# Attention backward beside a ReGLU: gradient products one slot behind the scores, another order of the first loads

## The chip, the cores and the metric

The kernel runs on one core of a Trainium2 chip. The metric is the device time of one execution in microseconds (us); the median of several runs is given. A core has five engines with instruction streams of their own, in the rows of the profile: PE (TensorE, matrix products; its weight loads are shown as PEld), DVE (VectorE), ACT (ScalarE), POOL (GpSimd) and SP (SyncE, which here only issues DMAs). `SPq` and `ACTq` are the DMA issues of SP and ACT.

## The reference

A gated mix of sliding-window attention and a ReGLU layer, forward and all gradients, in bfloat16. S = 2048 rows, D = 512, H = 32 heads of Dh = 16, window 256, F = 1376.

```python
g = sigmoid((x * gate_w).sum(-1, keepdims=True))
q, k, v = split(x @ wqkv)                             # 32 heads of 16
scores = q @ k.T * Dh**-0.5                           # per head; 0 <= i - j < 256, else -1e9
a = (softmax(scores) @ v) @ wo
b = (relu(x @ W_gate) * (x @ W_up)) @ W_down
out = g * a + (1 - g) * b
# returned: out and the gradients of x, wqkv, wo, W_gate, W_up, W_down, gate_w for a given grad_out
```

For the attention gradient one needs, for each block of queries and keys, P = exp(scores), the product dP = dO V^T, and P * dP (called Pd in the kernel), row sums of both, and both once more with rows and columns exchanged.

## The kernel before

**First stage (0 to about 250 us): the ReGLU.** A step is one chunk of 128 features (`fc`, 11 of them) for one group of 512 rows (`tg`, 4 of them): N1 = 44 steps. The loop over n runs 8 slots longer, and in slot n the parts of several steps are interleaved with a lag: `gate` and `up` of step n, `turn_h` of n - 1, `dh` of n - 2, stores of hT (`keep`) of n - 3, `turn_dgu` and stores of dgT and duT of n - 4, weight gradients of n - 6. `gate` makes a product in PSUM and ACT writes its ReLU to `rg` (L368); `up` makes a second product, from which DVE makes `upm` (L374) and POOL `hT` (L376); `dh` makes a third, which ACT copies (L382) and which DVE and POOL turn into the halves of `dgu` (L385, L386). `rg`, `upm`, `hT` and `dgu` go round in four buffers each. `keep` issues its three stores from ACT's queue (L399), and the transposes `turn_h` (L390) and `turn_dgu` (L394) are DMAs issued by SP. `turn_x` transposes the next group's x on PE. Before the loop SP issues the first loads in a written order: both halves of the first group of x, the first 128 columns of W_gate, the second group of x, gate_w, the first 128 columns of W_up, grad_out, and so on.

Near the end of this stage the projections of the first group of attention (Q, dO, K, V and their transposes; `project_parts`, L133 and L136 are its matmuls) are interleaved, and three parts of the second group (Q, dO, and the DMA transpose of their rows) at n = N1+4, N1+5, N1+6.

**Second stage (about 252 to 720 us): attention.** The work is a list of 360 units: for each of 4 column groups `c` (8 heads each) and 16 query blocks `j`, the key blocks j-1, j, j-2 (roles m, d, f: middle, diagonal, far), each in two halves of 4 heads. One slot of the loop does, by a written order, parts of several units:

- `front(units[n])`: the scores matmul ST (L680), its exp on ACT into `Pu` (L690), and for roles d and f the mask on POOL (L692, L695);
- `gradp(units[n - 1])`: the DVE product Pd = Pu * dPT (L709);
- `flip(units[n - 2])`: the exchange of rows and columns of P and Pd by a DMA transpose that SP issues (L737);
- `rowsum(units[n - LAG])`, LAG = 3: row sums into BA (L718, L720). Units without a DMA transpose are exchanged here on PE (L747) and copied out;
- `front_dp(units[n])`: the matmul dPT (L704), behind the row sums, or ahead of them where a new query block begins;
- then as credit allows `cd_piece` (L540, L543, the products with the exchanged P), parts of the next group's projections, and background products of the weight gradient (L634).

ST and dPT share a ring of four PSUM buffers:

```python
ST = ps.tile([P, HH, P], F32, tag="M", bufs=4, name="ST")
u.dPT = ps.tile([P, HH, P], F32, tag="M", bufs=4, name="dPT")
```

When the last row sum of a block is done, ACT copies BA (L724), and small operations follow on DVE (reciprocal L764) and POOL (ndel L767, rq L768 to L773, rows_st L775 to L782). `late` holds loads of weights for the last stage, `early` the first loads of attention gradients for it; the loop takes one of each now and then.

**Last stage (about 720 us to the end):** the outputs and the gradient of x, in 16 blocks of 128 rows (L1015 to L1098), on PE nearly all the time.

Of the kernel before, what the change touches and what calls it, by code (L numbers as in the profile page):

```python
# [11 lines left out]
BF = mybir.dt.bfloat16  # L12
# [10 lines left out]
def kernel(  # L23
# [20 lines left out]
    nc = tc.nc  # L44
    P = 128
# [152 lines left out]
    with ExitStack() as p1, tc.manual_schedule():  # L198
# [13 lines left out]
        def rows_of(ap, tg):  # L212
            return ap[tg * TGW:(tg + 1) * TGW, :].rearrange("(t p) d -> p t d", p=P)
# [28 lines left out]
        half = TPG // 2  # L242
        for i in range(2):
            nc.sync.dma_start(x_r[:, i * half:(i + 1) * half, :], rows_of(x_d, 0)[:, i * half:(i + 1) * half, :])
        gw_r = fp.tile([P, P], BF, tag="upm", name="gw_r")
        nc.vector.memset(tiny[:], 0.0)
        nc.vector.memset(gw_r[:], 0.0)
# [10 lines left out]
            nc.sync.dma_start(Wg_sb[:, :, a:b], Wg_v[:, :, a:b])  # L258
            nc.sync.dma_start(Wu_sb[:, :, a:b], Wu_v[:, :, a:b])

        nc.sync.dma_start(Wg_sb[:, :, 0:W0], Wg_v[:, :, 0:W0])
        load_x(1)
        nc.sync.dma_start(gw_r[0:DC, :], gate_w.rearrange("(c p) -> c p", p=P))
        nc.sync.dma_start(Wu_sb[:, :, 0:W0], Wu_v[:, :, 0:W0])
        load_go(0)
        nc.sync.dma_start(wd0[:], B_W_down[0:P, :])
        load_x(2)
# [89 lines left out]
        def tile1(tag, bufs=4):  # L357
            return fp.tile([P, TGW], BF, tag=tag, bufs=bufs, name=tag)
# [11 lines left out]
        def up(k):  # L370
            ups = ps1.tile([P, TGW], F32, tag="mm", bufs=3, name="ups")
            product(ups, lambda c: Wu_sb[:, c, k.fsl], lambda c: x_T[k.tg][:, c, :])
            k.upm, k.hT = tile1("upm"), tile1("hT")
            nc.vector.scalar_tensor_tensor(out=k.upm[:], in0=k.rg[:], scalar=0.0, in1=ups[:],  # L374
                                           op0=ALU.is_gt, op1=ALU.mult)
            nc.gpsimd.tensor_tensor(out=k.hT[:], in0=k.rg[:], in1=k.upm[:], op=ALU.mult)  # L376

        def dh(k):
            dhps = ps1.tile([P, TGW], F32, tag="mm", bufs=3, name="dhps")
            product(dhps, lambda c: WdT[k.fc][:, c, :], lambda c: db_T[:, c, k.ts])  # L380
            dh_sb = tile1("dh_sb", 2)
            nc.scalar.copy(dh_sb[:], dhps[:])  # L382
            k.dgu = fp.tile([P, 2, TGW], BF, tag="dgu", name="dgu")
            k.dgT, k.duT = k.dgu[:, 0, :], k.dgu[:, 1, :]
            nc.vector.tensor_tensor(out=k.dgT, in0=dh_sb[:], in1=k.upm[:], op=ALU.mult)  # L385
            nc.gpsimd.tensor_tensor(out=k.duT, in0=dh_sb[:], in1=k.rg[:], op=ALU.mult)  # L386
# [60 lines left out]
        for n in range(N1 + 8):  # L447
            at = lambda lag: steps[n - lag] if 0 <= n - lag < N1 else None
            if at(0):
                gate(at(0))  # L450
                if 0 < n < NTG:
                    gate_col(n)
                if n == 2:
                    turn_wd0()
                if n + 1 < NTG:
                    turn_x(n + 1)
                if n == 0:
                    turn_gw()
                up(at(0))
                if n == 0:  # L460
                    gate_col(n)
                if n < NTG:
                    db_rows(n)
                if at(0).tg == 0 and at(0).fc > 0:
                    turn_wd(at(0).fc)
            if 1 <= n <= NTG:
                turn_db(n - 1)
            if at(2):
                dh(at(2))
            if at(1):  # L470
                turn_h(at(1))
            if at(3):
                keep(at(3), (hT_d, at(3).hT[:]))
            if at(4):
                turn_dgu(at(4))
                keep(at(4), (dgT_d, at(4).dgT), (duT_d, at(4).duT))
            if at(6):
                f = weights(at(6))
                if f is not None:
                    stores[n + 1] = f  # L480
            if n in stores:
                stores.pop(n)()
            t = n - DA0
            if t % 2 == 1 and 0 <= t // 2 < NT:
                make_da(t // 2)
            if t % 2 == 0 and 0 < t // 2 <= NT:
                turn_da(t // 2 - 1)
            if t == 2:
                nc.vector.reduce_sum(par[:, 0:1], par4[:], axis=AX.X)
                nc.vector.tensor_scalar(par[:, 1:2], par[:, 0:1], -1.0, 1.0, op0=ALU.mult, op1=ALU.add)  # L490
            if n == NTG + 1:
                nc.scalar.activation(tiny[:], tiny[:], ACT.Exp)
            if t in (NT + 3, 2 * NT + 1):
                i = (t - NT - 3) // (NT - 2)
                nc.gpsimd.memset(zt[i][:, 0, :, :, :], 0.0)
                nc.vector.memset(zt[i][:, 1, :, :, :], 0.0)
            if n == N1 - 2:
                first = project_parts(*groups[0])
            for _ in range({N1 + 1: 2, N1 + 2: 0}.get(n, 1)):
                if first:  # L500
                    first.pop(0)()
            if n == N1 + 3:
                second = project_parts(*groups[1])
            if n in (N1 + 4, N1 + 5, N1 + 6):
                second.pop(0)()
            z = n - DA0 - NT - 2
            if z == 0:
                load_w(0)
            if z % 4 == 3 and 0 < z // 4 + 1 < DC:
                load_w(z // 4 + 1)  # L510

    p3 = ctx
    if True:
# [141 lines left out]
        for c in range(DC):  # L655
            for j in range(NT):
                kbs = [k for k in (j - 1, j, j - 2) if k >= 0]
                for half in range(2):
                    order = kbs if half or len(kbs) < 3 else [kbs[0], kbs[2], kbs[1]]
                    for ki, kb in enumerate(order):  # L660
                        u = Unit()
                        u.c, u.j, u.kb, u.half = c, j, kb, half
                        u.first = ki == 0 and half == 0
                        u.last = ki == len(kbs) - 1 and half == 1
                        u.role = ("d", "m", "f")[j - kb]
                        u.pair = u.role == "d" or (u.role == "m" and (c < DC - 1 or j in (3, 5, 7, 9)))
                        u.own = u.role == "f" or (u.role == "m" and half == 1 and not u.pair and j < 10)
                        u.dma = u.pair or (u.role == "m" and half == 0 and (c < DC - 1 or j < 10))
                        units.append(u)
        NU = len(units)  # L670
# [58 lines left out]
        def flip(u):  # L729
# [3 lines left out]
            if u.dma:  # L733
                if u.pair and u.half == 0:
                    return
                hs = slice(0, 2) if u.pair else slice(u.half, u.half + 1)
                nc.sync.dma_start_transpose(out=P2[key][:, hs, :, :, :].rearrange("p b a h q -> p (b a h) q"),  # L737
                                            in_=pairs.pop((u.c, u.j, u.kb))[:, hs, :, :, :].rearrange("p b a h q -> p (b a h q)"))
                for b in range(2)[hs]:
                    P2[(u.c, u.j, u.kb, b)] = P2[key][:, b, :, :, :]  # L740
                return
# [103 lines left out]
        with tc.manual_schedule():  # L845
# [3 lines left out]
            prq = []  # L849
            credit = 1.2  # L850
            SLOT = 1.5
            LAG = 3
            n = 0

            held = False
# [27 lines left out]
            while n <= NU + LAG or ev or cdq or bgq:  # L883
# [21 lines left out]
                for eng, f in now:  # L905
                    if eng == "pool":
                        f()
                if 1 <= n <= NU:
                    gradp(units[n - 1])
                for eng, f in now:  # L910
                    if eng == "dve":
                        f()
                for eng, f in now:
                    if eng == "pool+":
                        f()
                if 2 <= n < NU + 2 and units[n - 2].dma:
                    flip(units[n - 2])
                w = units[n - LAG] if LAG <= n < NU + LAG else None
                if u is not None and w is not None and w.first:
                    front_dp(u)  # L920
                    pieces()
                if w is not None:
                    rowsum(w)
# [2 lines left out]
                    if w.last:  # L926
# [5 lines left out]
                        for kb in done:  # L932
                            qbs = range(kb, min(NT, kb + 3))
                            for qb in qbs:
                                for half in range(2):
                                    e = n + (1 if qb < w.j else 5)
                                    cdq.append((e, w.c, kb, qb, half, qb == qbs[-1] and half == 1))
                if u is not None and not (w is not None and w.first):
                    front_dp(u)
                credit += SLOT - 0.63 - (0.44 if LAG <= n < NU + LAG and not units[n - LAG].dma else 0.0)  # L940
                if not (u is not None and w is not None and w.first):
                    pieces()
                if n >= NU:
                    if bgq:
# [20 lines left out]
                    credit -= 0.65  # L965
                if u is not None and u.c == DC - 1 and not bgq and u.j > 6 and "T0" not in S2:
                    early = early_group()
                if late and (u is None or u.c == 0 or (n % 12 == 1 and 3 <= u.j <= 8 if u.c < DC - 1 else
                                                       n % 4 == 1 and 1 < u.j < 10 or n % 2 and u.j > 9)):
                    late.pop(0)()  # L970
                if early and (u is None or n % 2 == 0 and u.j >= (9 if len(early) > 4 else 14)):
                    early.pop(0)()
                credit = max(-1.0, min(1.2, credit))
                for eng, f in now:
# [154 lines left out]
```

## Time and profile before

| | before |
|---|---|
| runs, us | 912.45, 912.24, 914.48 |
| median, us | 912.45 |
| the profiled execution, us | 913.61 |
| its span in the profile, us | 911.9 |
| granted TensorE clock | 1.00 |
| DMA, mean over the span | 185 GB/s |
| L704 dPT, 360 matmuls | 135.9 us, 378 ns each |
| L690 exp of the d units, 126 | 75.8 us, 601 ns each |
| L692 mask of the d units, 126 | 80.7 us, 641 ns each |
| L709 product of the d units, 126 | 85.8 us, 681 ns each |

The span is the part of the execution that the profile covers; what lies around it is 1.7 us here. In a line of the timeline the columns are start, duration, engine, source line, operation, output <- input, and in square brackets the idle time of the engine just before, with what ended it. In the list of waits they are the waiting operation, what ended the wait, the sum in us, the number of waits and the longest. Matmuls are pipelined: the next can begin before the bar of the previous one ends. Which event released a waiting instruction is inferred by the profile.

### The profile page before, as it was taken

How to read it: one execution, taken by the hardware profiler on the slowest of the kernel's cores; microseconds unless marked ns; L12 is line 12 of the kernel's file. 1: busy time of each engine (PE TensorE's matmuls, PEld its weight loads, DVE VectorE, ACT ScalarE, POOL GpSimd, SP SyncE). 2: the span in 40 equal slices, each digit the busy share in tenths (PEclk: the TensorE clock that was granted, in tenths of full speed). 3: DMA queues.
4: the chain of work that ended last, by engine and by line, in shares of the span. 5: the costliest groups of instructions: out<-in, count | busy, mean ns of one | idle time of the engine just before them, and what ended most of it. 6: DMA issues, size and time to landing. Idle time of an engine off the chain costs nothing.

```text
span 911.9 us, 26209 instructions
## 1 busy us (share of the span) xinstructions
PE 896.2 (98%) x10711; PEld 567.3 (62%) x10711; DVE 510.9 (56%) x952; ACT 441.6 (48%) x778; POOL 495.2 (54%) x937
## 2 busy tenths in 40 slices
PE   8999999999989999999999999999999999999998
PEld 5565665655647767667776677766777644444445
DVE  4433334434278877768777787776787222333333
ACT  6422222222268777667776677766688211000001
POOL 4554445545267777857878578875677212222221
PEclk9999999999999999999999999999999999999999
DMA  9989879999689999999999989999998999777731
GB/s 302 192 183 200 189 187 208 219 221 207 164 154 152 176 178 182 198 173 153 183 176 192 188 160 184 180 184 181 186 202 154 247 270 227 182 186 180 184 88 46
DMA packets 505577, 169.07 MB, mean 185 GB/s; under 512 B 433457, under 2 KB 504337, under 8 KB 505457
## 3 DMA queue, kind: packets, MB, share of 16 engines
q1 hardware_dynamic: 484816, 145.51, 85.7%
q10 hardware_dynamic: 19008, 17.31, 6.9%
q0 software_dynamic: 1632, 4.59, 1.4%
q8 instruction: 83, 1.36, 0.6%
q14 instruction: 38, 0.30, 0.1%
HBM read 32.28 MB, written 36.24 MB: 75 GB/s over the span
## 4 chain that ended last, share of the span: by engine, by line
PE 85%; POOL 6%; DVE 3%; DMA 2%; ACT 2%; issue 1%; SPq 1%; ACTq 0%; DVEq 0%; POOLq 0%
PE wps L411 8%; PE dxps L1054 8%; PE ST L680 7%; PE dPT L704 7%; PE pt L747 5%; PE dxps L1058 4%; PE dps L413 4%; PE pp L133 4%; PE bps L1027 4%; PE ups L362 4%; PE dhps L362 4%; PE wps L634 4%; PE gps L362 4%; PE BA L718 4%; PE CD L540 4%; PE CD L543 2%
## 5 line engine op out<-in xcount | busy, mean ns | idle before, releaser
L680 PE MATMUL ST<-z,K 128*128 128x512 bf16 x360 | 135.9, 378 | 2.7 <-DVE zT L74 0.9
L704 PE MATMUL dPT<-z,V 128*128 128x512 bf16 x360 | 135.9, 378 | 2.2 <-DVE PPd L709 1.1
L692 POOL TENSOR_SCALAR_AFFINE_SELECT PPd<-PPd 128x512 bf16<-128x512 bf16 x126 | 80.7, 641 | 104.0 <-ACT PPd L690 103.1
L709 DVE TENSOR_TENSOR Pd<-Pu,dPT 128x512 bf16<-128x512 bf16 x117 | 80.1, 684 | 61.9 <-POOL Pu L695 58.3
L376 POOL TENSOR_TENSOR hT<-rg,upm 128x512 bf16<-128x512 bf16 x44 | 51.2, 1164 | 115.6 <-DVE upm L374 89.3
L411 PE MATMUL wps<-dgu_r,x_r 128*128 128x256 bf16 (+1 forms) x704 | 103.9, 270 | 0.0
L709 DVE TENSOR_TENSOR PPd<-PPd,dPT 128x512 bf16<-128x512 bf16 x126 | 85.8, 681 | 17.7 <-POOL PPd L692 16.8
L411 PEld LDWEIGHTS <-x_r 128*128 128x128 bf16 x704 | 68.3, 98 | 30.6
L690 ACT ACTIVATE PPd<-ST 128x512 bf16<-128x512 f32 x126 | 75.8, 601 | 23.1 <-PE ST L680 22.7
L690 ACT ACTIVATE Pu<-ST 128x512 bf16<-128x512 f32 x117 | 70.2, 600 | 32.4 <-PE ST L680 32.3
L1034 ACT COPY a_sb<-aps 128x512 f32<-128x512 f32 x16 | 9.4, 586 | 151.4 <-issue 137.6
L690 ACT ACTIVATE PPm<-ST 128x512 bf16<-128x512 f32 x117 | 70.5, 603 | 24.5 <-PE ST L680 22.2
L695 POOL TENSOR_SCALAR_AFFINE_SELECT Pu<-Pu 128x512 bf16<-128x512 bf16 x112 | 73.9, 660 | 12.3 <-ACT Pu L690 11.6
L709 DVE TENSOR_TENSOR PPm<-PPm,dPT 128x512 bf16<-128x512 bf16 x117 | 78.1, 667 | 2.9 <-PE CD L543 1.0
L374 DVE SCALAR_TENSOR_TENSOR upm<-rg,ups 128x512 bf16<-128x512 bf16 x44 | 30.2, 686 | 80.2 <-PE ups L362 47.8
L72 ACT COPY p<-pt 128x1024 bf16<-128x1024 bf16 x67 | 68.3, 1020 | 3.8
L368 ACT ACTIVATE rg<-gps 128x512 bf16<-128x512 f32 x44 | 26.3, 597 | 88.1 <-PE gps L362 42.0
L413 PE MATMUL dps<-db_r,h_r 128*128 128x512 bf16 x176 | 66.7, 379 | 0.0
L386 POOL TENSOR_TENSOR dgu<-dh_sb,rg 128x512 bf16<-128x512 bf16 x44 | 57.7, 1311 | 5.1 <-ACT dh_sb L382 5.1
L1040 POOL DMA_DIRECT2D out_dram<-o_sb x16 | 8.7, 543 | 87.7 <-DVE o_sb L1038 81.3
L634 PE MATMUL wps<-rows_st,x_r 128*128 128x384 bf16 x256 | 50.3, 325 | 0.1
L385 DVE TENSOR_TENSOR dgu<-dh_sb,upm 128x512 bf16<-128x512 bf16 x44 | 32.0, 727 | 32.7 <-ACT dh_sb L382 29.1
(193 smaller groups left out, 2375.3 us busy)
## 6 DMA issues: line engine op xcount, KB each, us to landing
dqkvo_d<-rows_st SPq DMA_DIRECT2D x15, 512.0 KB, 3.9
hT_d<-hT ACTq DMA_DIRECT2D x44, 128.0 KB, 2.2
dgT_d<-dgu ACTq DMA_DIRECT2D x44, 128.0 KB, 3.0
duT_d<-dgu ACTq DMA_DIRECT2D x44, 128.0 KB, 2.9
duT_g<-duT_d SPq DMA_DIRECT2D x8, 640.0 KB, 5.3
gt<-hT_d SPq DMA_DIRECT2D x7, 640.0 KB, 5.7
dgT_g<-dgT_d SPq DMA_DIRECT2D x7, 640.0 KB, 5.3
out_dram<-wst SPq DMA_DIRECT2D x20, 128.0 KB, 2.5
```

The lines of the kernel that those rows point to most:

```text
L72: nc.scalar.copy(out, in_)
L362: nc.tensor.matmul(out[:], lhsT=w(c), rhs=x(c), start=(c == 0), stop=(c == DC - 1))
L411: nc.tensor.matmul(acc["w"][:, c, 0:2 * nw], lhsT=x_r[:, t, c * P:(c + 1) * P], rhs=k.dgu_r[:, :, i, s0:P], start=(go_ and c % 2 == 0), st ...
L413: nc.tensor.matmul(acc["d"][:], lhsT=k.h_r[:, i, :], rhs=db_r[:, t, :], start=go_, stop=no_)
L634: nc.tensor.matmul(wps[:], lhsT=x_r[:, t, part * P:(part + 1) * P], rhs=sts[c][:, t, 0:3, :], start=first and t == t0, stop=last and t == ...
L680: nc.tensor.matmul(ST[:], lhsT=KTt[:, ksl], rhs=z[:, 0, :, jl, :], start=True, stop=True)
L690: nc.scalar.activation(u.Pu[:], ST[:], ACT.Exp)
L692: nc.gpsimd.affine_select(out=u.Pu[:], in_=u.Pu[:], compare_op=ALU.is_ge, fill=0.0, base=0, pattern=[[0, HH], [1, P]], channel_multiplier=-1)
L695: nc.gpsimd.affine_select(out=u.Pu[:], in_=u.Pu[:], compare_op=ALU.is_ge, fill=0.0, base=-1, pattern=[[0, HH], [-1, P]], channel_multiplier=1)
L704: nc.tensor.matmul(u.dPT[:], lhsT=VTt[:, ksl], rhs=z[:, 1, :, jl, :], start=True, stop=True)
L709: nc.vector.tensor_tensor(out=u.Pd[:], in0=u.Pu[:], in1=u.dPT[:], op=ALU.mult)
L1054: nc.tensor.matmul(to, lhsT=src[:, fc, lsl], rhs=W6[(wt, fc)][:, cols], start=(fc == 0 and wt == "Wg"), stop=False)
```

## The change

The attention loop takes `dPT` of the unit before (n - 1) in place of the unit whose scores are made, the DVE product of unit n - 2, the DMA transposes of unit n - 3, and row sums of unit n - 4. For the last four slots of the list and three slots behind it (`calm`), no load of `late` or `early` is taken. Middle units of the last column group that are exchanged on PE now keep P and Pd in the pair buffers and no longer in buffers of their own (`own`, `pairs`). In the first stage the load of the first columns of W_gate stands between the halves of x, that of W_up ahead of the second group of x; `up` stands ahead of `turn_x`; hT has seven buffers, dgu six; the three parts of the second group run at N1+2, N1+3, N1+4. In the file after, the lines of the functions named are one to three further down.

```diff
@@ first loads
         for i in range(2):
             nc.sync.dma_start(x_r[:, i * half:(i + 1) * half, :], rows_of(x_d, 0)[:, i * half:(i + 1) * half, :])
+            if i == 0:
+                nc.sync.dma_start(Wg_sb[:, :, 0:W0], Wg_v[:, :, 0:W0])
...
-        nc.sync.dma_start(Wg_sb[:, :, 0:W0], Wg_v[:, :, 0:W0])
+        nc.sync.dma_start(Wu_sb[:, :, 0:W0], Wu_v[:, :, 0:W0])
         load_x(1)
         nc.sync.dma_start(gw_r[0:DC, :], gate_w.rearrange("(c p) -> c p", p=P))
-        nc.sync.dma_start(Wu_sb[:, :, 0:W0], Wu_v[:, :, 0:W0])
         load_go(0)
@@ up, dh
-            k.upm, k.hT = tile1("upm"), tile1("hT")
+            k.upm, k.hT = tile1("upm"), tile1("hT", 7)
...
-            k.dgu = fp.tile([P, 2, TGW], BF, tag="dgu", name="dgu")
+            k.dgu = fp.tile([P, 2, TGW], BF, tag="dgu", bufs=6, name="dgu")
@@ loop of the first stage
+                up(at(0))
                 if n + 1 < NTG:
                     turn_x(n + 1)
                 if n == 0:
                     turn_gw()
-                up(at(0))
...
-            if n == N1 + 3:
+            if n == N1 + 2:
                 second = project_parts(*groups[1])
-            if n in (N1 + 4, N1 + 5, N1 + 6):
+            if n in (N1 + 2, N1 + 3, N1 + 4):
                 second.pop(0)()
@@ units and flip
-                        u.own = u.role == "f" or (u.role == "m" and half == 1 and not u.pair and j < 10)
+                        u.own = u.role == "f"
...
-                                            in_=pairs.pop((u.c, u.j, u.kb))[:, hs, :, :, :].rearrange("p b a h q -> p (b a h q)"))
+                                            in_=pairs[(u.c, u.j, u.kb)][:, hs, :, :, :].rearrange("p b a h q -> p (b a h q)"))
@@ loop of the second stage
-            LAG = 3
+            LAG = 4
...
-                if 1 <= n <= NU:
-                    gradp(units[n - 1])
+                if 2 <= n <= NU + 1:
+                    gradp(units[n - 2])
...
-                if 2 <= n < NU + 2 and units[n - 2].dma:
-                    flip(units[n - 2])
+                if 3 <= n < NU + 3 and units[n - 3].dma:
+                    flip(units[n - 3])
                 w = units[n - LAG] if LAG <= n < NU + LAG else None
-                if u is not None and w is not None and w.first:
-                    front_dp(u)
+                v = units[n - 1] if 1 <= n <= NU else None
+                if v is not None and w is not None and w.first:
+                    front_dp(v)
                     pieces()
                 if w is not None:
                     rowsum(w)
...
-                if u is not None and not (w is not None and w.first):
-                    front_dp(u)
+                if v is not None and not (w is not None and w.first):
+                    front_dp(v)
...
-                if late and (u is None or ...
+                calm = not NU - 4 < n < NU + 3
+                if late and calm and (u is None or ...
...
-                if early and (u is None or ...
+                if early and calm and (u is None or ...
```

More of the change, by code (lines that the diff above doesn't have):

```diff
@@ L937 @@
                                     cdq.append((e, w.c, kb, qb, half, qb == qbs[-1] and half == 1))
-                if u is not None and not (w is not None and w.first):
-                    front_dp(u)
+                if v is not None and not (w is not None and w.first):
+                    front_dp(v)
                 credit += SLOT - 0.63 - (0.44 if LAG <= n < NU + LAG and not units[n - LAG].dma else 0.0)
-                if not (u is not None and w is not None and w.first):
+                if not (v is not None and w is not None and w.first):
                     pieces()
@@ L967 @@
                     early = early_group()
-                if late and (u is None or u.c == 0 or (n % 12 == 1 and 3 <= u.j <= 8 if u.c < DC - 1 else
+                calm = not NU - 4 < n < NU + 3
+                if late and calm and (u is None or u.c == 0 or (n % 12 == 1 and 3 <= u.j <= 8 if u.c < DC - 1 else
                                                        n % 4 == 1 and 1 < u.j < 10 or n % 2 and u.j > 9)):
                     late.pop(0)()
-                if early and (u is None or n % 2 == 0 and u.j >= (9 if len(early) > 4 else 14)):
+                if early and calm and (u is None or n % 2 == 0 and u.j >= (9 if len(early) > 4 else 14)):
                     early.pop(0)()
```

## The prediction, made before the changed kernel was run

> **What bounds it now.** I began with the totals and the forty slices, to see which engine sets the time and where it does not.
>
> ```profile
> PE 896.2 (98%) x10711; PEld 567.3 (62%) x10711; DVE 510.9 (56%) x952; ACT 441.6 (48%) x778; POOL 495.2 (54%) x937
> PE   8999999999989999999999999999999999999998
> ```
>
> TensorE (PE) is the bound: 911.9 - 896.2 = 15.7 us idle. The change leaves its work alone (21,424 matmuls and weight loads before and after), so only idle time can be won. A 512-column matmul is drawn 0.38 us long though the next can start 0.215 us later, so up to 0.16 us of a wait hides under a bar. Taking start-to-start times on the timeline less the spacing of an undisturbed matmul (512 columns 0.215, 384 0.162, 128 0.055, the small BA and CD ones 0.025) I get 22.8 us of waiting:
>
> - 0 to 30 us: 6.4, of which 2.1 stand at 29.7;
> - 250 to 270: 5.9, the start of attention;
> - 280 to 690: 8.8, in about fifty pieces of at most 0.4;
> - 700 to 722: 1.5. Between 32 and 250 and from 722 to 908 there is none.
>
> The waits of PE, then the stretch table (length, then busy time of PE, weight loads, DVE, ACT, POOL) name them:
>
> ```profile
> PE gps L362 <- ACT rg L368: 1.9, 1, 1.9
> PE dPT L704 <- DVE PPd L709: 1.1, 2, 0.9
> PE ST L680 <- DVE zT L74: 0.9, 1, 0.9
> PE CD L540 <- DMA p2d<-PPd: 0.7, 1, 0.7
> ...
> 250.00:270.00 20.00, 15.79 (x192) 8.94 (x190) 15.18 (x30) 13.27 (x25) 11.52 (x27) 1.00 0.81 145
> ...
> 280.00:690.00 410.00, 407.75 (x7185) 289.39 (x7184) 316.28 (x594) 299.98 (x535) 303.68 (x699) 1.00 1.08 179
> ```
>
> In the long stretch DVE is 77%, ACT 73% and POOL 74% busy: none is the bound, each is late now and then. The timeline shows how:
>
> ```profile
> 349.38 0.64 ACT L690 ACTIVATE PPd<-ST 128x512 bf16<-128x512 f32 x1
> 350.09 0.64 POOL L692 TENSOR_SCALAR_AFFINE_SELECT PPd<-PPd 128x512 bf16<-128x512 bf16 x1 [1.49 <-ACT PPd L690]
> 350.76 0.69 DVE L709 TENSOR_TENSOR PPd<-PPd,dPT 128x512 bf16<-128x512 bf16 x1 [0.51 <-POOL PPd L692]
> 351.50 0.38 PE L704 MATMUL dPT<-z,V 128*128 128x512 bf16 x1 [0.23 <-DVE PPd L709]
> ```
>
> exp, mask and product follow one another, and the product frees the PSUM buffer that the next dPT needs. PE's previous matmul began at 351.09, a small one: 0.41 - 0.025 = 0.38 us lost. Of the 8.8 us, 5.1 end right behind a DVE product, 1.3 behind an exp, 1.45 are CD waiting for POOL's rq (L773), and most of the rest is ACT's rows_st (0.4) and a DVE copy (0.3).
>
> **Part 1: dPT one slot behind, products two, row sums four.** Nothing is added; matmuls, products and transposes move. A slot is 456 us / 360 units = 1.27 us, the shortest 0.83. Before, dPT is written beside its own scores and holds one of four shared PSUM buffers through exp (0.60), mask (0.64 or 0.66) and product (0.68): 1.9 to 2.4 us. After, it is written a slot later with the product a slot behind it, by when the mask is mostly done: about 1.1 us. At two matmul outputs a slot the mean occupancy falls from some 2.3 to 1.7 of four. The largest product wait (0.39) is a third of a slot, so nearly all 5.1 should go. DVE still works in order: at the seven changes of column group it has bursts of copies (z, K, V: 0.51, 0.58, 1.03 us near 367) ahead of products; for each I leave 0.11, 0.8 in all. Term: **-4.3**. The exp, rq and rows_st waits keep their relative order, so I take nothing there. Bounds: -7.5, all but the rq waits; -1, if DVE's bursts and not the mask set most of them.
>
> The new waits: row sums (BA) still come two slots behind their product, as before. SP's DMA transposes of P come one slot later. The smallest spare time before is 4.35 us from landing to the CD that reads it, 3.54 us from landing to the exp that rewrites the source; both exceed 1.27, price 0. The PE transposes write to a ring whose slot lag moves with LAG, price 0. If this cover were gone, each missing microsecond would be PE's.
>
> **Part 2: start of attention, 250 to 270.** Second-group Q and dO move two steps forward, the same 8 matmuls and copies. ST no longer waits for the zT copy (0.9 row; 1.04 by spacing), but the K projection behind it now waits for a bank that ACT (0.48) and then DVE (0.56) empty at the end of the weight-gradient stage, so far covered by dO's 0.86 us of matmuls: about 0.93 comes back. From 262 the chain runs through POOL's masks and small products (0.64, 0.21, 0.40, 0.40, 0.40, 0.41 us), unchanged. Walking POOL's queue in the new order, the BA that starts at 269.37 starts near 269.15, with one more ST ahead of it: **-0.4**. Bounds +0.5 (bank wait uncovered, nothing won on POOL) and -1.3 (the zT wait and the first masks both gone). Rows transposes go to SP two steps earlier, into time in which it has none of the early loads to delay.
>
> **Part 3: head.** Loads of Wg before the second x half and Wu before x1 shift PE by -0.4 to +0.3 near 14 us. Whatever comes of it is swallowed at 29.7, where gate waits for an rg buffer. Moving `up` ahead of `turn_x` changes order only. The listing blames POOL, and the change gives hT 7 and dgu 6 buffers, which would take that wait away:
>
> ```profile
> 30.79 0.47 ACTq L399 DMA_DIRECT2D duT_d<-dgu  x1
> 31.37 0.60 ACT L368 ACTIVATE rg<-gps 128x512 bf16<-128x512 f32 x1 [3.20 <-POOL hT L376]
> ```
>
> But rg reads gate's PSUM and not hT; its buffer was read long before. On ACT it stands behind the three stores (issued 29.27, 30.43, 30.79), which start as earlier transposes land (29.25, 30.41), behind the Wg and Wu loads. 30.79 + 0.47 = 31.26, then rg at 31.37. The bytes ahead are the same after: **0**. Bounds +0.3, and -2.1 if POOL's label is right (a rival). The Trainium skill ("TensorE: Matmul & The Clock Gate", Architectural detail) says ACT and DVE are strict FIFO and that only PE pulls anything ahead; by that rule the term is 0, by the label it is -2.1, and the 31.26 beside 31.37 agrees with the rule.
>
> **Part 4: end of attention.** Two waits stand here: 0.52 at 708.5 (BA behind the last product) and 0.84 at 719.4 (CD behind the last transpose, issued 714.16, landed 720.24). Its product was done at 707.6; SP is busy without a break with loads queued ahead of it. `calm` holds late and early loads back: one goes ahead of 693.9 where SP idles 2.4 us, and the last transpose comes some 2 us earlier, so the 0.84 goes; about 0.4 of the 0.52 goes because weight-gradient matmuls stand between. Term **-1.2**, bounds 0 and -1.4. The delayed loads landed at 708.9 and 716 and are needed at 722 or later; a slot or two costs 0 while the 6 us hold. The pairs/own edits change buffers for ten blocks, 0.
>
> **Sum.** -4.3 - 0.4 + 0 - 1.2 = -5.9. The profiled execution took 913.61 (span 911.9 and 1.7 around it): 907.7. It lies 1.16 above the median of the runs, 912.45; from that, 906.5 us.
>
> **Rivals.**
>
> *Little is won.* The product waits are DVE's and POOL's bursts, seen one slot later, and the other end of each bound holds: -1.0 + 0.5 - 0.5 = -1.0, 911.4 us. For it: the waits repeat at the same place in every column group (436, 464, 551, 580). Against: 0.38 us of delay against 1.27 of room.
>
> *More is won.* POOL's label at 31.37 is right, and looser buffers take the exp waits as well: -(5.1 + 1.3) - 0.4 - 1.2 - 2.1 = -10.1, 902.3 us. For it: exp's wait is for the same ring of four. Against: ACT's issue order at 31.26.
>
> *Slower: late transposes.* SP issues them in order among loads, and DMA in this stretch shows a share of 1.08. One slot later, the smallest spare 4.35 becomes 3.1; it decides once landing (2.3 to 3.4 us after issue) stretches by more than that. Then the first CD of each of the 64 (column group, query block) pairs waits. At the 0.2 us of the shortest CD wait listed that is 12.8: 912.45 - 5.9 + 12.8 = 919.4 us. Against: only one such wait exists before, in the drain.
>
> *It does not do what it says.* The four buffers go round in program order, so a scores matmul could take over the wait that dPT loses, with DVE no earlier: 0 to -0.5, 912.2 us.
>
> **How the numbers follow.** Forecast 0.48 (own range 904.5 to 909.5), more 0.22, little 0.15, nothing 0.06, slower 0.09. A measurement here can tell about 0.3%, 2.7 us: faster means below 909.7, slower above 915.2. Forecast and more give 0.70, plus 0.03 from little with a somewhat larger steady gain: faster 0.73; slower 0.09 and 0.02 for unpriced bounds: 0.11; same 0.16. The range 901.5 to 912.0 takes in steady -7.5 with the label's 2.1 at one end and most of little at the other; about 0.2 lies outside.
>
> **What would show it.** Right: PE idle falls from 15.7 to about 11; the waits of dPT and ST for products nearly vanish in 280 to 690 while CD's wait for rq stays; gate's wait for rg near 29.7 stays at about 1.9; BA starts near 269.2 and ST's wait for zT is gone; CD's wait for p2d is gone. Wrong: rg's wait gone (part 3), waits moved to ST behind exp or to BA behind products (part 1), CD waiting for transposes in mid-stage (the slower case), or PE's rows longer than 0.38.

## The result: 0.34% slower, and the profile after

The changed kernel took 915.79 us (median of 15 runs, 912.87 to 919.77) against 912.57 for the kernel before on the same chip (15 runs, 911.27 to 915.73): a ratio of 1.0034, 95% interval 1.0019 to 1.0049. A second group of 12 runs on another occasion gave 914.89 against 913.41, 1.0022 (1.0006 to 1.0037). The forecast was 906.5 and a range of 901.5 to 912.0: wrong in sign. The profiled execution took 913.90 (span 912.2), one of the quicker ones, so its trace alone does not hold the whole loss.

The totals of the page:

```profile
PE 890.6 (98%) x10611; PEld 566.6 (62%) x10711; DVE 510.9 (56%) x952; ACT 441.4 (48%) x778; POOL 493.2 (54%) x937
```

The waits of PE:

```profile
PE BA L719 <- ACT BAs L725: 1.9, 1, 1.9
...
PE ST L681 <- DVE PPm L710: 1.2, 2, 0.6
PE ptd L327 <- DVE x L74: 1.2, 2, 0.7
PE CD L541 <- DMA p2d<-PPd: 0.9, 1, 0.9
PE pp L133 <- DVE wst_end L74: 0.8, 1, 0.8
```

The stretches of the start of attention and of the steady part, with the columns as before:

```profile
250.00:270.00 20.00, 16.13 (x182) 8.95 (x181) 12.67 (x25) 12.59 (x24) 11.14 (x26) 1.00 0.73 121
...
280.00:690.00 410.00, 404.21 (x7158) 289.11 (x7204) 319.77 (x594) 301.70 (x536) 302.14 (x701) 1.00 1.08 179
```

First a caution: 10,611 matmuls stand beside 10,711 weight loads, so 100 matmul records are missing here. They lower PE's busy time by records and not by waiting. Where two weight loads lie between two recorded matmuls, I count 0.216 us, the spacing of a matmul of 512 columns, for the missing one. With that rule the waiting of PE by start-to-start times is, in us:

| stage | before | after |
|---|---|---|
| 0 to 12 | 4.2 | 3.7 |
| 12 to 32 | 2.2 | 2.4 |
| 32 to 250 | 0.0 | 0.7 |
| 250 to 272 | 5.9 | 6.3 |
| 272 to 690 | 8.8 | 7.7 |
| 690 to 722 | 1.5 | 2.1 |
| the rest | 0.2 | 0.2 |
| sum | 22.8 | 23.1 |

The sum agrees with the spans (911.9 and 912.2). Nothing was won in all. The waits stand in other places: BA behind ACT's copy, ST behind products, PE transposes behind DVE's copies of x, a projection behind a copy of DVE (`wst_end`); CD still waits for the last transpose, and the wait of gate for rg near 30 us is not in the list any more. Two things stay to be found: where the expected 5.9 us went, and why the median lies 2 us above the profiled execution.

### The profile page after: what moved, and what is told of

It reads as the page before. It is cut to its first block, busy times and chain, and to the rows that moved or that the text cites. A ratio compares the mean times of both kernels' runs of the same rounds, so it can differ in the third digit from the quotient of the medians.

```text
span 912.2 us, 26028 instructions
## 1 busy us (share of the span) xinstructions
PE 890.6 (98%) x10611; PEld 566.6 (62%) x10711; DVE 510.9 (56%) x952; ACT 441.4 (48%) x778; POOL 493.2 (54%) x937
## 4 chain that ended last, share of the span: by engine, by line
PE 82%; DVE 5%; DMA 3%; issue 3%; POOL 3%; ACT 2%; SPq 1%; POOLq 0%; DVEq 0%; ACTq 0%
PE dxps L1057 8%; PE ST L681 8%; PE dPT L705 7%; PE wps L412 7%; PE pt L748 6%; PE dxps L1061 4%; PE bps L1030 4%; PE CD L541 4%; PE BA L719 4%; PE wps L635 4%; PE dhps L363 4%; PE pp L133 3%; PE gps L363 3%; PE ups L363 3%; PE dps L414 3%
## 5 line engine op out<-in xcount | busy, mean ns | idle before, releaser
L696 POOL TENSOR_SCALAR_AFFINE_SELECT Pu<-Pu 128x512 bf16<-128x512 bf16 x112 | 72.0, 643 | 31.6 <-ACT Pu L691 30.5
L710 DVE TENSOR_TENSOR Pd<-Pu,dPT 128x512 bf16<-128x512 bf16 x112 | 76.3, 682 | 21.6 <-POOL Pu L696 11.1
L710 DVE TENSOR_TENSOR PPm<-PPm,dPT 128x512 bf16<-128x512 bf16 x122 | 81.5, 668 | 7.8 <-PE dPT L705 6.1
L691 ACT ACTIVATE Pu<-ST 128x512 bf16<-128x512 f32 x112 | 67.4, 602 | 34.2 <-PE ST L681 33.6
L691 ACT ACTIVATE PPm<-ST 128x512 bf16<-128x512 f32 x122 | 73.7, 604 | 20.1 <-PE ST L681 19.5
L414 PE MATMUL dps<-db_r,h_r 128*128 128x512 bf16 x159 | 60.3, 379 | 0.0
L133 PE MATMUL pp<-x,p 128*128 128x512 bf16 x152 | 44.7, 378 | 2.7 <-DVE wst_end L74 0.8
```

The costliest lines, as they stand in the source:

```text
L133: nc.tensor.matmul(pp[:], lhsT=w_p[c][:, cd, which * P:(which + 1) * P], rhs=x_T[tg][:, cd, :], start=(cd == 0), stop=(cd == DC - 1))
L414: nc.tensor.matmul(acc["d"][:], lhsT=k.h_r[:, i, :], rhs=db_r[:, t, :], start=go_, stop=no_)
L691: nc.scalar.activation(u.Pu[:], ST[:], ACT.Exp)
L696: nc.gpsimd.affine_select(out=u.Pu[:], in_=u.Pu[:], compare_op=ALU.is_ge, fill=0.0, base=-1, pattern=[[0, HH], [-1, P]], channel_multiplier=1)
L710: nc.vector.tensor_tensor(out=u.Pd[:], in0=u.Pu[:], in1=u.dPT[:], op=ALU.mult)
```

## The experiments

### The parts, one by one

`slot_only` makes the attention loop's edits alone (dPT, gradp, flip, LAG, calm, own and pairs); `head_only` the first loads, `up` ahead of `turn_x` and the buffers; `second_only` the move of the second group's three parts. `after_again` is the changed kernel itself.

> The changed kernel once more, unaltered. First theory (waits): PE's waiting is about the same in every execution, 23 us as in the profiled one, so this profile has a span near 912 and the times spread little; the 3.2 us of the medians are then not explained. Second theory (clock): the executions differ in granted clock (0.994 to 1.000 in the runs so far), each 0.001 of clock goes with about 1 us, and runs at 0.999 to 1.000 lie at 913 to 915, those at 0.994 to 0.996 at 917 to 920; a profile with a clock of 0.997 or less would show where the clock was lost.

> The kernel before with the attention loop's part alone: dPT, products, transposes and row sums one slot later, calm, buffers of the pairs. My step of the prediction: 5.5 us faster than before (4.3 in the steady stretch, 1.2 at its end). First theory (waits, from the profile after): steady stretch 1.1 less waiting, end 0.5 more, start of attention unchanged: 0.5 us faster. Second theory (clock): if this part brings the clock loss, 2 to 4 us slower than before, with clocks under 0.999 in most runs.

> The kernel before with the part of the first 250 us alone: order of first loads, up ahead of turn_x, hT seven and dgu six buffers. My step: 0 (-0.4 to +0.3), the 2.1 us wait for rg at 29.7 stays. First theory (waits, from the profile after): that wait goes and about as much appears between 9 and 20 us, 0.38 and 0.21 appear at 159 and 240: 0.4 us slower. Second theory (clock): if this part brings it, 2 to 4 us slower with clocks under 0.999.

> The kernel before with the second group's Q and dO two steps forward and nothing else. My step: 0.4 us faster. First theory (waits): the 0.94 at 251.3 (K projection for a bank) takes the place of ST's 1.04, no more than 0.5 us either way. Second theory (clock): if the denser or sparser start of attention brings the clock loss, 2 to 4 us slower with clocks under 0.999.

| kernel | median, us | ratio to before, 95% | executions with a mean granted clock of 0.998 or less |
|---|---|---|---|
| after_again | 914.89 | 1.0022 (1.0006 to 1.0037) | 9 of 12 |
| slot_only | 912.47 | 0.9993 (0.9982 to 1.0005) | 10 of 12 |
| head_only | 915.37 | 1.0018 (1.0006 to 1.0030) | 2 of 12 |
| second_only | 914.39 | 1.0006 (0.9994 to 1.0019) | 3 of 12 |

The first 15 runs of the changed kernel had 11 such executions; the kernel before, over its four groups of runs, 17 of 132. So there are two causes. The head costs 1.6 us (1.8 thousandths of 913) without the clock; second_only is not told apart from the kernel before. The loop's part is not slower in the median but lowers the clock in most executions. The profile of slot_only shows where; these are four windows of it (the third figure from the right is the granted clock):

```profile
261.60:265.01 3.41, 3.29 (x50) 2.12 (x49) 1.98 (x3) 3.08 (x5) 3.33 (x9) 1.00 1.37 161
265.01:268.42 3.41, 1.54 (x34) 1.18 (x32) 2.74 (x5) 1.30 (x3) 3.01 (x8) 1.00 1.18 223
268.42:271.83 3.41, 3.19 (x35) 1.80 (x34) 0.69 (x1) 1.89 (x3) 2.84 (x8) 0.50 1.16 215
271.83:275.24 3.41, 3.36 (x59) 2.20 (x59) 2.12 (x4) 1.58 (x4) 2.01 (x5) 1.00 1.18 129
```

On its timeline, two dPT matmuls inside the third window and a score matmul behind it:

```profile
268.67 0.63 PE L704 MATMUL dPT<-z,V 128*128 128x512 bf16 x1
...
270.00 0.59 PE L704 MATMUL dPT<-z,V 128*128 128x512 bf16 x1
...
274.81 0.38 PE L680 MATMUL ST<-z,K 128*128 128x512 bf16 x1
```

A window in which PE is busy for 1.54 of 3.41 us is followed by one at half clock, in which a matmul of 512 columns lasts 0.6 us instead of 0.38. The sparse window holds one wait, of BA for ACT's copy of an earlier BA:

```profile
266.52 0.40 POOL L782 TENSOR_TENSOR rows_st<-BAs,rinv 128x128 bf16<-128x128 f32 x1
266.95 0.49 ACT L724 COPY BAs<-BA 128x400 f32<-128x400 f32 x1 [2.17 <-POOL rows_st L782]
267.50 0.18 PE L718 MATMUL BA<-KV,PPm 128*128 128x33 bf16 x1 [1.86 <-ACT BAs L724]
```

The kernel before waits at the same place for 0.7 us only, and loses the rest earlier in smaller pieces:

```profile
265.42 0.38 PE L704 MATMUL dPT<-z,V 128*128 128x512 bf16 x1 [0.85 <-DVE PPd L709]
...
269.37 0.18 PE L718 MATMUL BA<-KV,PPm 128*128 128x33 bf16 x1 [0.71 <-ACT BAs L724]
```

A clock of 0.998 is one such window in 913 us. Measured by executions at 0.998 against full ones of the same kernel, one window goes with 1.9 us in after_again (915.30 against 913.41) and 2.8 us in before (915.80 against 913.03); over all kernels it is 1.1 (slot_wo_later, 912.46 against 911.33) to 3.3 (before beside slot_relief, 916.57 against 913.28), by medians of a few executions each. Half of 3.41, 1.7 us, is the most that one half-clock window can take by itself; the remainder was not traced.

### Which edit of the head

> The kernel before with up ahead of turn_x in the first slots and nothing else. Head theory: this order brings the waits of PE for DVE's copies of x (0.65 to 0.85, twice) and for rg (0.67) between 12 and 20 us, 2.2 us in all, and takes about 1 us off the later wait for rg at 29: 1 to 2 us slower than before, as head_only was (1.7). Rival (loads): the order of loads makes them, and this one is within 0.5 of before.

> The kernel before with the other order of the first loads and nothing else. Head theory (up): within 0.5 us of before, with only the wait for the second half of x changed. Rival (loads): 1 to 2 us slower, with the waits between 12 and 20 us.

> The kernel before with seven hT and six dgu buffers and nothing else. By my step (ACT's issue order) the wait of gate for rg at 29 us stays at 0.9 to 2.1 and the time is that of before. By the profile's label (POOL's hT) the wait goes and the kernel is 1 to 2 us faster.

up_only 915.10, ratio 1.0023 (1.0014 to 1.0032); loads_only 912.44, 0.9992 (0.9983 to 1.0000); bufs_only 913.28, 1.0002 (0.9992 to 1.0012). It is the order of `up`: 2.1 us (2.3 thousandths). The trace of the changed kernel tells how, DVE first and then PE:

```profile
13.02 0.68 DVE L375 SCALAR_TENSOR_TENSOR upm<-rg,ups 128x512 bf16<-128x512 bf16 x1
13.62 0.68 DVE L74 COPY x<-ptx 128x1024 bf16<-128x1024 bf16 x1
...
14.36 1.05 PE L327 MATMUL ptd<-ident,db_r 128*128 128x128 bf16 x16 [0.68 <-DVE x L74]
17.40 1.02 PE L363 MATMUL ups<-x,Wu_sb 128*128 128x512 bf16 x4 [0.51 <-ACT rg L369]
19.81 1.22 PE L327 MATMUL ptd<-ident,db_r 128*128 128x128 bf16 x16 [0.49 <-DVE x L74]
```

With `up` first, DVE makes upm before it empties the transposes of x, and the next transposes wait for their PSUM buffer. Nothing of turn_x any longer stands between gate and up, and up waits for what the transposes had covered. These three waits are 2.2 us by start-to-start times. In exchange the later wait of gate for rg near 30 us is gone in all four profiles with `up` first (after, after_again, head_only, up_only). The balance therefore hangs on how large that later wait would have been. It is 2.0 to 2.1 us in the profiles of before and slot_early0, 0.7 to 1.2 in ten others, and absent in after_three. By the start of the first weight-gradient matmul, the four stand at 34.3 to 35.3 us and eleven of the thirteen others at 32.8 to 33.6; the two exceptions are before (34.6) and slot_early0 (33.9). So the profiled execution of before hid the cost of `up`, and the medians show it.

bufs_only settles the label of the wait at 29 us. hT has seven buffers there and POOL no longer waits for a store, yet gate's wait for rg stays; rg still follows ACT's stores:

```profile
29.36 0.36 ACTq L399 DMA_DIRECT2D duT_d<-dgu  x1
29.82 0.60 ACT L368 ACTIVATE rg<-gps 128x512 bf16<-128x512 f32 x1 [2.26 <-PE dhps L362]
30.46 1.02 PE L362 MATMUL gps<-x,Wg_sb 128*128 128x512 bf16 x4 [1.00 <-ACT rg L368]
```

The size of this wait is not the kernel's: unchanged heads showed 2.1 (before), 0.9 (slot_only) and 1.2 (second_only).

### The large wait and the clock

```diff
-            at = (6, 7, 12, 13) if j == 0 else (4, 5, 6, 7)
+            at = (5, 6, 10, 11) if j == 0 else (4, 5, 6, 7)                              # slot_early0
+            at = (6, 7, 12, 13) if j == 0 else (4, 5, 5, 5) if c == 0 and j == 1 else (4, 5, 6, 7)   # slot_relief
```

> The attention loop's part alone (as slot_only), with the small POOL operations of each first query block (j = 0) earlier by one and two slots: at slots 5, 6, 10, 11 behind its last row sum in place of 6, 7, 12, 13. They release the copy of BA that the third block's copy waits for. Clock theory: the 1.9 us wait of BA for ACT's copy near 266 makes one 3.41 us window with less than 0.30 of its time in streamed columns, and the next window then runs at half clock, in 10 of 12 executions. With the wait at 0.5 or less no window falls under 0.33, clocks of 0.998 and less become as rare as in the kernel before (6 of 35), and the median falls by 1.4 from the clock and by up to 1.5 from the wait, 912.5 to 909.5 - 911. Rival: the whole start of attention is sparse enough and its place does not matter; the clock is then still at 0.998 or less in most executions and the median gains at most the wait.

> The attention loop's part alone (as slot_only), with the last three small POOL operations of the second query block (c = 0, j = 1) ahead of two masks in place of behind them. The copy of BA that PE waits for near 266 stands behind the second block's rows_st, not the first's, which moving the first block's operations (slot_early0) showed. Clock theory: the BA wait falls from 1.9 to 0.6 or so (two masks of 0.64 us less in front of it), no 3.41 us window stays under 0.33 of streamed columns, half-clock windows become as rare as in the kernel before (9 of 70), and the median falls from 912.5 to 910 - 911. Rival: the whole start is sparse enough and its one large wait does not matter: clocks of 0.998 and less stay in most executions, and the median gains 1 us or less.

slot_early0 missed its aim: the wait grew from 1.9 to 2.7 us. The copy waits for the second block's rows_st, and the first block's operations now ran ahead of that. With the larger wait 10 of 11 executions lost clock (10 of 12 in slot_only); the median is 913.78, 1.0011 (0.9999 to 1.0023). slot_relief, aimed at the second block, cut the wait to 0.8:

```profile
PE CD L540 <- DMA p2d<-PPd: 1.1, 1, 1.1
PE ST L680 <- DVE zT L74: 0.9, 1, 0.9
PE BA L718 <- ACT BAs L724: 0.8, 1, 0.8
```

Median 911.88, 0.9982 (0.9962 to 1.0002), and 5 of 12 with a lowered clock: better than 10, worse than expected. Its profile shows a second place, the wait for the last transpose at the end of attention:

```profile
716.10:719.50 3.40, 2.21 (x53) 1.64 (x53) 0.15 (x2) 0.79 (x3) 0.00 (x0) 1.00 0.77 210
719.54:722.95 3.41, 3.41 (x13) 1.58 (x11) 1.38 (x4) 0.48 (x1) 0.96 (x1) 0.50 0.75 211
```

### The last transpose

```diff
-                if late and calm and (u is None ...
+                if late and calm and (late[0] is not load_wo or n >= NU + 3) and (u is None ...
```

> The attention loop's part alone, with the four loads of wo behind the last transpose of P in place of ahead of it on SP. Queue theory: in the changed kernel the last transpose is issued 2 us earlier than before (712.2 against 714.2) but lands at the same time (720.5 against 720.2), because 1 MB of loads and a store is under way ahead of it; without the wo loads in front it lands 1 us or more earlier and CD's wait for it near 719 (1.04 in the changed kernel) falls under 0.3. Rival: the 512 KB store of rows_st right ahead of it holds it, whatever the loads do: no change of that wait.

911.54 us, 0.9973 (0.9959 to 0.9986), 4 of 12 with a lowered clock. The first sparse place is untouched here: its profile has a half-clock window at 270.25, behind the wait of BA (1.89). In the changed kernel the last transpose was issued 2 us earlier than before, as predicted, and landed no earlier. Most of the 2 us is that the loop itself ended earlier: the last scores matmul starts at 704.79 against 706.17. Counted from it, the issue came 0.6 us earlier (7.4 against 8.0) and the landing 1.6 us later. The issue and the CD that waits for it, before and then in the changed kernel:

```profile
714.16 2.89 SPq L737 DMA_TRANSPOSE p2d<-PPd  x1
...
720.29 0.19 PE L540 MATMUL CD<-rq,p2d 128*128 128x32 bf16 x1 [0.69 <-DMA p2d<-PPd]
```

```profile
712.22 4.56 SPq L738 DMA_TRANSPOSE p2d<-PPd  x1
...
720.52 0.19 PE L541 MATMUL CD<-rq,p2d 128*128 128x32 bf16 x1 [0.89 <-DMA p2d<-PPd]
```

It took 8.25 us from issue to landing (720.47); before, 6.08. With wo's loads behind it, it took 6.22 (709.05 to 715.27) and CD did not wait for it:

```profile
708.42 0.53 SPq L561 DMA_DIRECT2D dqkvo_d<-rows_st  x1
709.05 3.80 SPq L737 DMA_TRANSPOSE p2d<-PPd  x1
```

slot_only's own profile has no such wait either, so one profile does not decide it, but all of them agree: with the new loop and the loads in front it took 7.3 to 8.5 us in seven profiles, and CD waited 0.5 to 2.2 us in six of them; with the loads behind (slot_wo_later, best, after_three, before_both) it took 5.6 to 6.2 and CD never waited. The store of rows_st stayed in front, so the store alone does not hold it. Nor do the loads alone: in the loop of before, the same loads and the same store are issued ahead of it, the store first, and it took 6.1 to 6.5 us in all six profiles. There the four loads come last, and in the changed kernel the store, 0.5 us ahead; whether that order makes the difference was not tested.

### The waits behind products

```diff
-  ev.setdefault(n + 1 + k, []).append(("dve", lambda gi=gi, k=k: spread(gi + 1, k)))
+  ev.setdefault(n + 1 + 2 * k, []).append(("dve", lambda gi=gi, k=k: spread(gi + 1, k)))
```

> The attention loop's part alone, with DVE's four z copies of the next column group in every second slot in place of four slots in a row. Order theory: in the steady stretch PE's waits behind DVE products are 5.4 us with the change (3.6 before) because a product now stands in DVE's order behind z copies and K, V scalings and no mask holds it; with the copies apart they fall to 3.5 to 4.5, the waits of 0.76 at 480 and 596 to under 0.4, and the kernel is 1 to 2 us faster than slot_only. Rival: the four PSUM buffers are what is short, whatever DVE does first; the waits stay within 0.5 of 5.4.

To compare the steady stretch (275 to 690) I put each wait down to the operation that ended 20 to 130 ns ahead, with one rule for all kernels. It gives, in us:

| ended by | before | slot_only, and after | slot_spread2 |
|---|---|---|---|
| DVE product | 3.6 | 5.4 | 1.5 |
| ACT exp | 2.6 | 1.1 | 5.1 |
| POOL rq | 1.5 | 0.1 | 0.1 |
| others | 1.0 | 1.1 | 3.8 |
| sum | 8.7 | 7.7 | 10.4 |

The other profiles of each loop agree to 0.4 (sums 8.3 to 8.7 and 7.6 to 7.8). The order theory was right on the products: spreading the z copies cuts their waits from 5.4 to 1.5. It was wrong on the time: 915.90 us, 1.0025 (1.0007 to 1.0043). Exp and copies took the waits over, and their sum rose by 2.7. Why exp became the late one was not followed further; that the engines take turns at the four buffers fits both columns.

### All of it together

`best` is slot_only with the other first loads and both repairs; `before_both` the kernel before with the repairs; `after_three` the changed kernel with `up` back and both repairs. `after_up_back` only puts `up` back.

> The changed kernel with up behind turn_x again, as before, and everything else changed. Head theory: 2.0 to 2.2 us faster than the changed kernel, about 913 (what up_only added to before), with the waits for DVE's x copies between 12 and 20 us gone. Rival: in the company of the other edits the order of up is hidden or needed, within 0.7 of the changed kernel.

> The attention loop's part and the other order of first loads, with both repairs (the second block's small POOL operations ahead of two masks; wo's loads behind the last transpose), and without up ahead of turn_x, the buffers and the second group's move. Clock theory: neither the start of attention (near 268) nor its end (near 719) leaves a 3.41 us window under 0.38, so at least 10 of 12 executions have a clock of 0.999 or 1.000, and the median is that of the full-clock runs of the parts, 909.5 to 910.5 (slot_relief 910.6, slot_wo_later 911.3, loads -0.5). Rival: the clock drops for another reason and the share of runs under 0.999 stays at a third or more; median 911 to 912.

> The kernel before with the two repairs alone (one mask behind the second block's last small POOL operation; wo's loads behind the last transpose). If the repairs carry the gain by themselves: 911.5 or less, as slot_wo_later. If the loop's part carries it (1.1 us less waiting in the steady stretch, 0.5 at the end): 912 to 913, with only the 0.7 of CD's wait for the last transpose and a few tenths of the BA wait gone.

> The changed kernel with three edits: up behind turn_x again and both repairs. If the three causes (order of up, clock at 268, clock and wait at 719) make up its loss: 910 to 911, within 0.7 of best. If the second group's early Q and dO cost something of their own: 0.5 to 1 more than best, from PE's 0.9 us wait for a bank near 251.

| kernel | median, us | ratio to before, 95% | clock 0.998 or less |
|---|---|---|---|
| after_up_back | 914.02 | 1.0013 (0.9996 to 1.0030) | 8 of 12 |
| after_three | 910.91 | 0.9981 (0.9971 to 0.9991) | 0 of 11 |
| best | 910.37 | 0.9975 (0.9966 to 0.9984) | 0 of 10 |
| before_both | 912.00 | 0.9993 (0.9982 to 1.0004) | 0 of 11 |

after_up_back lies 0.9 to 1.8 us under the two medians of the changed kernel, a little less than the 2.0 expected; its profile had a 2.0 us wait for the last transpose. With the two sparse places repaired no execution of 32 had a clock of 0.998 or less. For best and after_three that is telling: they ran on the chip of slot_early0, where the new loop lost clock in 10 of 11. For before_both it is not, since the kernel beside it lost clock in 2 of 27 only. Three edits turn the changed kernel's loss into a gain of 1.7 us (1.9 thousandths). before_both does not reach best, so the loop's part is worth something: 912.00 - 910.37 = 1.6 us, with the loads' order in it. The second group's move and the buffers (after_three against best, 0.5) are not told apart from nothing.

## Why the prediction was wrong, step by step

**Head, priced at 0.** Right for the loads and for the buffers, within the intervals; the FIFO rule of the Trainium skill ("TensorE: Matmul & The Clock Gate", Architectural detail) gave the buffers 0, and bufs_only agrees with 1.0002. The step that failed is "Moving `up` ahead of `turn_x` changes order only": it was priced without walking DVE's and PE's queues, and measured 2.1 us. The sentence ahead of it failed too: whatever comes is "swallowed at 29.7". That wait was 2.1 us in the one profile read, but 0.7 to 1.2 in most others, and there was too little of it to swallow the 2.2 us of new waits. The sign "rg's wait gone" came true through `up`, not through the label that it was meant to test.

**Steady stretch, -4.3.** This is the largest failed term. "Nearly all 5.1 should go" took the mask to be what makes the product late. In the changed kernel the mask seldom holds it, yet the waits behind products grew. The page shows the first for the products of the far units, before and after; the last figures are DVE's idle time in front of them and the part that a mask ended:

```profile
L709 DVE TENSOR_TENSOR Pd<-Pu,dPT 128x512 bf16<-128x512 bf16 x117 | 80.1, 684 | 61.9 <-POOL Pu L695 58.3
...
L710 DVE TENSOR_TENSOR Pd<-Pu,dPT 128x512 bf16<-128x512 bf16 x112 | 76.3, 682 | 21.6 <-POOL Pu L696 11.1
```

DVE's order is what is left (the product behind a z copy, then the score matmul, whose predecessor on PE began at 480.39):

```profile
480.17 0.42 DVE L120 COPY z<-zT 32x1024 bf16<-32x1024 bf16 x1
480.62 0.69 DVE L710 TENSOR_TENSOR PPm<-PPm,dPT 128x512 bf16<-128x512 bf16 x1
...
481.36 0.38 PE L681 MATMUL ST<-z,K 128*128 128x512 bf16 x1 [0.60 <-DVE PPm L710]
```

I left 0.8 us for such bursts, and 5.4 us of waits stand behind products. 3.9 of these went (and others came) when the z copies were spread, which puts most of them down to the copies. The waits that I priced at no change, exp and rq, fell by 1.5 and 1.4. Together -1.0 instead of -4.3, just at the end of my bounds. The split of the 8.8 us into 5.1, 1.3 and 1.45 was loose too: the one rule used above gives 3.6, 2.6 and 1.5. (The 21,424 matmuls and weight loads are 21,422 on the page; nothing hangs on it.)

**Start of attention, -0.4.** The sum of waiting came out at +0.4, inside the bounds but of the other sign. The bank wait of 0.93 came as told (0.94), and POOL's chain set the end, with BA at 270.4 and not at 269.2. What I did not see is that a sum of waits does not tell their effect: the same waiting gathered in one wait of 2.0 us makes a window sparse enough for the clock to halve. The prediction has no term for the clock; every row of before that it read showed 1.00.

**End, -1.2.** The issue came 2 us earlier as told, though mostly because the loop ended earlier. That an earlier issue is an earlier landing was the false step; the transpose took 8.25 us in place of 6.08, with loads and a store issued in the 3 us ahead of it. Profiled +0.6.

**The rivals.** The "late transposes" case was right in kind at one place, the last one, and wrong in the place and size it was priced for (64 waits in mid-stage). "Little is won" came nearest for the steady stretch. None had the clock or `up` in it. The bounds that "little" names add up to -1.0 + 0.5 + 0.3 + 0 = -0.2, 912.25 us, and not to the -1.0 written there; no case but the late transposes was slower. Of the signs for being right one came, the end of ST's wait for zT.

The account: `up` 2.1; the clock about 1.2; the loop's waiting, with the other order of the loads, about -1.6 (best against before_both). That is +1.7, against 3.2 and 1.5 in the two groups of runs. The clock's part is worked out in the second group: the changed kernel loses 1.5 us from its executions at 0.999 or more to all of them (913.41, three only, to 914.89), the kernel before 0.3 (913.08 to 913.41). In the first group the changed kernel loses 1.6. The parts overlap within their intervals and no closer account can be made.

## What to carry to other kernels

Walk the queue of every engine for an edit that "only changes order", above all where two producers share PSUM buffers through one in-order engine. Count not only how much PE waits but how it is spread: a wait that is gathered in one place can cost more than the same waiting in pieces, and here only the granted clock of several executions showed it. A wait that is to swallow another should be read from more than one profile. When a wait behind one engine is taken away in a ring of shared buffers, expect the next engine in the ring and look for a gain in the sum, not in that row.

## What the runs showed of the hardware

The granted clock halved for 3.41 us at a time inside the kernel though PE was never idle for more than 2.7 us on end (slot_early0), and for no more than 0.5 us in the window ahead of the drop in slot_spread2. In the 17 profiles I cut PE's time into windows of 3.41 us from the first change of the clock, and took the share in which columns stream (0.417 ns a column, 0.213 us for 512, just under their spacing of 0.215). Windows at 0.34 or less (five: 0.15, 0.30, 0.30, 0.31, 0.34) were each followed by a half-clock window; at 0.36 one was and one was not; from 0.38 on none was. Where the windows fall differs from execution to execution (the first change came at 4.0 to 10.5 us), which fits that the same program loses clock in some and not in others; the windows were read in the profiled executions only. The Trainium skill ("TensorE: Matmul & The Clock Gate", What's actually happening) gives the window as 3413 ns and free-running, and names an idle window as what brings the half clock. The first agrees: in slot_only the drop at 268.42 lies 77 windows behind the change at 5.59. The second asks for more than it took here, where windows that streamed for a third of their time were followed by half clock too.

A DMA transpose of the same size took 5.6 to 8.5 us from issue to landing at the end of attention, by what was issued in front of it and when (before_both 5.55, before 6.1, changed kernel 8.25, slot_relief 8.5).
